# Moving a row norm with its read-back, one output product and the last output tile in a two-layer attention and gMLP kernel

## The chip, the cores and the metric

The kernel runs on one core of a Trainium2 chip. The metric is the device time of one execution in microseconds (us); less is better. Times are medians over several executions, and one execution is recorded by the hardware profiler.

In what follows PE is the matrix engine, DVE the vector engine, ACT the scalar engine, POOL the GpSimd engine and SP the engine whose queue issues most of the transfers. "L905" is line 905 of the kernel before the change.

## The reference

Two blocks are run twice over a sequence x of 2048 rows of 512 values, both as residuals. Block A is a recurrent attention with memory: 64 segments of 32 rows, each attending to itself and to 8 memory rows, which are the first 8 output rows of the segment before. Block B is a gated MLP with a spatial mixing over all 2048 rows.

```python
def A(x, mem, Wq, Wk, Wv, Wo):               # 32 heads of 128
    for s in range(64):
        h = concat([mem, x[32*s:32*s+32]])   # 40 rows
        q, k, v = h @ Wq, h @ Wk, h @ Wv
        o = softmax(mask(q @ k.T / sqrt(128))) @ v @ Wo
        mem = o[:8]; out.append(o[8:])
    return concat(out)

def B(x, w_in, w_sp, b_sp, w_out):
    z = gelu(x @ w_in)                       # 2048 x 1376
    g = w_sp @ layernorm(z[:, 688:]) + b_sp[:, None]
    return (z[:, :688] * g) @ w_out

x = x + A(layernorm(x));  x = x + B(layernorm(x))
x = x + A(layernorm(x));  x = x + B(layernorm(x))
```

## The kernel before

Four stages follow each other: `a_block` (first), `b_block`, `a_block`, `b_block` (last, which writes the output). Inside both, the order of the instructions on PE, DVE and ACT is the order of the code; in `b_block` SP's order is too, while in `a_block` SP's transfers are placed by a scheduler.

**Attention.** `segment(s, fill, spare1, spare2, tail)` issues one segment of 32 rows. Rows come in 16 blocks of 128 (`tb = s // 4`), so a block has four segments (`j4 = s % 4`). A segment projects its 40 rows (`hA`, transposed on DVE at L782) to q, k and v on PE, copies the results out of PSUM on ACT (L828, L844), transposes them on DVE (L832, L847), computes the scores, their exponentials (ACT, L872) and the masking (DVE, L875), the product with v (`psO`, L891) and the row sums (`psD`, L946). The memory rows are divided by their sums first (`uT<-psO,Rm`, L958) and multiplied with Wo (`pw`, L724), because the next segment needs them: `build_hA` puts them into the next segment's rows (L781) and transposes (L782). The other rows follow (`tok_out`, L905) once ACT has the reciprocal sums (`Rt`, L964). `fill()` puts matmuls of other work (the projections of each segment's last 8 rows, `b_units`, and earlier output products, `y_part`) into the places where PE would wait. The number of PE instructions of a segment is padded to a fixed multiple (`pads_of`).

Between these stand two places for work of other rows. `spare1` is called after the masking (L875) and ahead of L958, `spare2` after L958 and ahead of `tok_out`. In `spare1` stands the residual sum of an earlier row tile (`rows.y_add`), in `spare2` its statistics and the row norm of the tile two blocks ahead:

```python
                if j4 == 3 and tb + 2 < NB:
                    rows.apply(tb + 2, MV_in, RS_in, first=first)
```

`rows.apply` (L196) normalises 128 rows on DVE (L201) into `ln_xn`, stores them to `xn_d` in DRAM (L203), and reads them back in two layouts: four transfers into `preB` (L206) for `ahead.turn` and four tiles `pre` (L213), one for each segment of that block. It runs in 14 segments of each attention block. `rows.load` reads the rows for the next such call into the one buffer `ln_x`.

**gMLP.** `b_block` projects all 16 row tiles (`project`), normalises, and then mixes: `gate(t, sts)` multiplies the spatial weights of tile t (`wspT`, loaded transposed by `load_wsp` through SP) with all 16 row tiles, in two parts of 10 and 6 row tiles, 20 and 12 matmuls. `product(t)` multiplies the sum with the other half on DVE (L390), starts the load of the spatial weights of tile t + 3, transposes the product by a transfer (L394) to `uT[t]`, and loads the rows of tile t - 1 for the residual. `finish(t)` is the output product: six matmuls of 128x512 (L407), the residual sum on DVE (L412 in the last block, L415 in the first) and the store. PSUM tiles: `gate` uses `pg0` and the two slots of `two`, `finish` and `turn_u` the two slots of `one`. The sums `xo` have two buffers. `turn_u` transposes the last product on PE and copies it on ACT (L402), instead of by a transfer. The loop is

```python
        for t in range(3, NT):
            gate(t, range(0, 10))
            finish(t - 3)
            gate(t, range(10, NT))
            product(t)
```

and after it `finish(13)`, `turn_u(15)`, `finish(14)`, `finish(15)`.

Of the kernel before, what the change touches and what calls it, by code (L numbers as in the profile page):

```python
# [8 lines left out]
F32 = mybir.dt.float32  # L9
ACT = mybir.ActivationFunctionType  # L10
ALU = mybir.AluOpType
# [3 lines left out]
P = 128  # L15
DM = 512
# [20 lines left out]
def _perm(ap):  # L37

    return ap.rearrange("p (cg kt el) -> p kt cg el", cg=4, kt=4, el=32)


def _nat(ap):
    return ap.rearrange("p (kt cg el) -> p kt cg el", kt=4, cg=4, el=32)
# [77 lines left out]
def _rstd_act(nc, out, var, c):  # L121
    nc.scalar.activation(out=out, in_=var, func=ACT.Ln, bias=c["eps_t"][:], scale=1.0)
    nc.scalar.activation(out=out, in_=out, func=ACT.Exp, scale=-0.5)
# [19 lines left out]
def _stats(nc, pool, x_tile, MV_out_slot):  # L143
    st = pool.tile([P, nc.vector.BN_STATS_DIM], F32, name="bnst")
    nc.vector.bn_stats(out=st[:], in_=x_tile)
    nc.vector.bn_aggr(out=MV_out_slot, in_=st[:])
# [94 lines left out]
def b_block(tc, c, rows, front, xd, MV_out, RS_out, w_sp, w_out, S, first, ahead, wo, out_final=None):  # L241

    nc = tc.nc
    NT = S // P
    ident_bf = c["ident_bf"]
    with ExitStack() as ctx:

        def sbuf(name, stack=ctx, bufs=1):
            return stack.enter_context(tc.tile_pool(name=name, bufs=bufs))

        w_in_sb = front.w_in_sb
        w_out_sb = sbuf("b_w_out").tile([P, 6, DM], BF16, name="w_out_sb")
# [9 lines left out]
        xt, wsp = {}, {}  # L262

        def z(tt, lo=0, hi=FF):
            return zs[tt >= 6][:, tt - 6 * (tt >= 6), lo:hi]
# [99 lines left out]
        two = _Tagged(ps_pool, "two", 2)  # L365
        one = _Tagged(ps_pool, "one", 2)
# [3 lines left out]
        pg, u, uT, rstds = {}, {}, {}, []  # L370
        n = 6 * P
        us = [front.take(n * i, n) for i in range(2)]
# [4 lines left out]
        def gate(t, sts):  # L377
            if sts[0] == 0:
                pg[t] = (two if t % 3 else pg0).tile([P, 2, 512], F32, name="pg")
            for st in sts:  # L380
                for k in range(2):
                    nc.tensor.matmul(pg[t][:, k, 0:344], lhsT=wsp[t][:, st, :], rhs=z(st, 344 * k, 344 * k + 344),  # L382
                                     start=(st == 0), stop=(st == NT - 1))

        def product(t):
            del wsp[t]
            if t + 3 < NT:
                load_wsp(t + 3)
            u[t], uT[t] = us[t % 2], uTs[t % 3]
            nc.vector.scalar_tensor_tensor(out=u[t][:, 0:FH].rearrange("p (k f) -> p k f", k=2), in0=pg.pop(t)[:, :, 0:344],  # L390
                                           scalar=c["bsp"][:, t:t + 1], in1=z(t, FH).rearrange("p (k f) -> p k f", k=2),
                                           op0=ALU.add, op1=ALU.mult)
            if t + 1 < NT:
                nc.sync.dma_start_transpose(out=uT[t], in_=u[t].rearrange("t (fc s) -> t fc s", s=P))  # L394
            if t > 0:
                load_x(t - 1)

        def turn_u(t):
# [2 lines left out]
                nc.tensor.transpose(pT[:, fc * P:(fc + 1) * P], u[t][:, fc * P:(fc + 1) * P], ident_bf[:])  # L401
            nc.scalar.copy(uT[t].rearrange("p fc r -> p (fc r)"), pT[:, 0:n])  # L402

        def finish(t):
            py = one.tile([P, DM], F32, name="py")
            for fc in range(6):
                nc.tensor.matmul(py[:], lhsT=uT[t][:, fc, :], rhs=w_out_sb[:, fc, :], start=(fc == 0), stop=(fc == 5))  # L407
            xs = xt.pop(t)
            xo = gp.tile([P, DM], F32, name="xo")
            if out_final is not None:  # L410
                xob = xo[:, 0:DM // 2].bitcast(BF16)
                nc.vector.tensor_tensor(out=_nat(xob), in0=_nat(py[:]), in1=_perm(xs[:]), op=ALU.add)  # L412
                nc.sync.dma_start(out_final[t * P:(t + 1) * P, :], xob)
                return
            nc.vector.tensor_tensor(out=_perm(xo[:]), in0=_nat(py[:]), in1=_perm(xs[:]), op=ALU.add)  # L415
            nc.sync.dma_start(xd[t * P:(t + 1) * P, :], xo[:])
            _stats(nc, gp, xo[:], MV_out[:, t, :])
            rstds.append(lambda: _rstd_act(nc, RS_out[:, t:t + 1], MV_out[:, t, 1:2], c))
            if t < 2:
                rstds.pop()()  # L420
                rows.apply(t, MV_out, RS_out, x=xo[:], eng=nc.gpsimd)
            elif len(rstds) > 1:
                rstds.pop(0)()

        for t, sts, done in ((0, range(0, 10), False), (1, range(0, 10), False), (0, range(10, NT), True), (2, range(0, 10), False),
                             (1, range(10, NT), True), (2, range(10, NT), True)):
            gate(t, sts)
            if done:
                product(t)
        for t in range(3, NT):  # L430
            gate(t, range(0, 10))
            finish(t - 3)
            gate(t, range(10, NT))
            product(t)
            if t == NT - 2 and out_final is None:
                ahead.begin()
# [174 lines left out]
def a_block(tc, c, rows, front, MV_in, RS_in, MV_out, RS_out, ahead, wo, S, first):  # L611
    nc = tc.nc
    NSEG = S // SEG
    NB = S // P
# [3 lines left out]
    with ExitStack() as ctx:  # L618
# [55 lines left out]
        uT = [pers.tile([P, H, 32], BF16, name=f"uT{i}") for i in range(2)]  # L674
# [5 lines left out]
        def ln_turn(tb):  # L680
            blk_state[tb] = dict(hB=ahead.turn(tb), KTB=KTBr[tb % 2], QTB=QTBr[tb % 2], VB=VBr[tb % 2])
# [79 lines left out]
        def y_stats(tb):  # L761
            rows.y_stats(tb, MV_out[:, tb, :])
            copies.append(lambda: _rstd_act(nc, RS_out[:, tb:tb + 1], MV_out[:, tb, 1:2], c))
# [234 lines left out]
        def values(units):  # L998
            for n in (3, 1):
                for _ in range(n):  # L1000
                    next(units)
                run(copies)
                yield

        for s in range(NSEG):
            tb, j4 = s // 4, s % 4
            if j4 == 0:
                q = tb % 4
                more = y_part(tb // 4 - 1, range(8 * q, 8 * q + 8), (1, 2, 4), 4, q == 0, q == 3) if tb > 3 else iter(())
            if first and s == 0:  # L1010
                more = values(units)
            if j4 > 0 and tb == NB - 1:
                n = [sum(k) for k in TAIL_HEADS]
                stops = [sum(TAIL_HEADS[j4 - 1][:k]) for k in (1, 2, 3)]
                more = y_part(tb // 4, range(sum(n[:j4 - 1]), sum(n[:j4])), stops, 3, j4 == 1, j4 == 3)
            elif j4 == 1:
                more = b_units(tb + 1)
            if j4 == 1 and tb + 2 < NB:
                rows.load(tb + 2, first, nc.sync)

            def spare1():
                if first and s == 1:
                    ln_turn(1)
                if ys:
                    rows.y_add(ys[0], first, nc.vector, nc.sync)
                if s == NSEG - 1:
                    rows.y_load(due[0], first, nc.sync, rows.pool.tile([P, DM], F32, name="y_x")[:],
                                rowsB[:].rearrange("p a n -> p (a n)").bitcast(F32))()

            def spare2():  # L1030
                if first and s == 0:
                    rows.apply(1, MV_in, RS_in, first=True)
                if first and s == 8:
                    c["cast_bsp"] = c["load_bsp"]()
                if first and s == 12:
                    c["cast_bsp"]()
                if ys:
                    y_stats(ys[0])
                if j4 == 2 and tb + 2 < NB and first:
                    _stats(nc, rows.pool, rows.xs[tb + 2], MV_in[:, tb + 2, :])  # L1040
                    copies.append(lambda: _rstd_act(nc, RS_in[:, tb + 2:tb + 3], MV_in[:, tb + 2, 1:2], c))
                if j4 == 3 and tb + 2 < NB:
                    rows.apply(tb + 2, MV_in, RS_in, first=first)

            def tail():
                if j4 == 0 and tb + 1 < NB and not (first and s == 0):
                    ln_turn(tb + 1)
                if tb == NB - 1:
                    front.load_w(j4)
                    if j4 > 0:  # L1050
                        front.load_rows(j4 - 1)
                if ys:
                    y_norm(ys.pop(0), nc.sync)
                if tb % 4 == 3 and j4 == 0 and tb > 4:
                    due.extend(range(tb - 7, tb - 3))

                if due and (j4 != 3 or tb + 2 >= NB) and s < NSEG - 1:
                    ys.append(due.pop(0))
                    rows.y_load(ys[0], first, nc.sync)()

            segment(s, lambda: next(more, None), spare1, spare2, tail)
# [7 lines left out]
        for h in range(H):  # L1069
            n = h // 8 * 8 + 2 * (h % 4) + h // 4 % 2  # L1070
            for k in range(4):
                nc.tensor.matmul(pw[32 * k:32 * k + 32, 0:256], lhsT=ends[k // 2][:, n, :],
                                 rhs=wo.head(h).rearrange("p (kt g el) -> p g kt el", kt=4, g=4)[:, k % 2 * 2:k % 2 * 2 + 2],
                                 start=(h == 0), stop=(h == H - 1), tile_position=(0, 32 * k))
# [46 lines left out]
```

## Time and profile before

| | |
|---|---|
| median of 4 runs | 1775.41 us (1767.29 to 1777.56) |
| the profiled execution's own time | 1775.67 us |
| its span, first to last instruction | 1772.8 us |
| mean granted TensorE clock | 0.998 |
| first gate to the moved product, first gMLP | 802.4 to 819.5 us |
| the same in the last gMLP | 1672.6 to 1689.7 us |
| start of the last output sum (DVE L412) | 1769.36 us |

A row of the timeline gives the start, the duration, the engine, the line, the operation, the tiles with their shapes, the number of instructions merged into the row, and in brackets how long the engine had been idle and what released it. A row of the waits gives the total, the number and the longest. A row of the windows gives a stretch, its length, the busy time of PE, PEld (the weight loads), DVE, ACT and POOL with their numbers of instructions, the granted clock, the busy share of the transfer engines and GB/s.

### The profile page before, as it was taken

Reading aid. Unit: us, or ns where it says so; the run is one execution under the profiler, and the core shown is the slowest. Engines: PE = TensorE matmul, PEld = TensorE weight load, DVE = VectorE, ACT = ScalarE, POOL = GpSimd, SP = SyncE. Lnnn points to the kernel's source line nnn. Section 1 sums busy time; section 2 is a strip of 40 time slices with the busy share of each in tenths; the row PEclk is TensorE's granted clock in tenths of the full one; section 3 lists DMA queues with packets and bytes.
Section 4 is the critical chain, followed back from the end, with each engine's and each line's share of the span. In section 5 each row is a group of like instructions: output and inputs, shape, how many; then the busy total and the mean of one; then the engine's idle time right before and its main releaser. Section 6 shows DMA issues by size and latency. Waiting matters only on the chain.

```text
span 1772.8 us, 109760 instructions
## 1 busy us (share of the span) xinstructions
PE 1704.3 (96%) x51164; PEld 1275.5 (72%) x51164; DVE 1159.2 (65%) x2861; ACT 1110.3 (63%) x2274; POOL 121.9 (7%) x274
## 2 busy tenths in 40 slices
PE   2999999999999999999999999999999999999999
PEld 1677777777777777756667777777777777777565
DVE  2666666687667766775366666666776677666723
ACT  1677777777777777661057777777777777766500
POOL 6000000000000000021100000000000000001100
PEclk9999999999999999999999999999999999999999
DMA  9200000021002102277940000001210131114697
GB/s 353 65 20 20 20 20 20 20 73 44 18 17 67 54 25 42 80 161 162 208 138 23 23 21 23 23 23 41 80 38 23 35 89 42 31 30 144 136 184 171
DMA packets 191818, 124.53 MB, mean 70 GB/s; under 512 B 135961, under 2 KB 168057, under 8 KB 191361
## 3 DMA queue, kind: packets, MB, share of 16 engines
q1 hardware_dynamic: 182656, 90.37, 21.5%
q0 software_dynamic: 8688, 27.14, 4.6%
q8 instruction: 399, 6.54, 1.6%
q14 instruction: 59, 0.48, 0.1%
q10 hardware_dynamic: 16, 0.01, 0.0%
HBM read 57.06 MB, written 33.53 MB: 51 GB/s over the span
## 4 chain that ended last, share of the span: by engine, by line
PE 92%; DMA 3%; DVE 2%; issue 1%; POOL 1%; ACT 0%; DVEq 0%; SPq 0%; POOLq 0%
PE psm L667 14%; PE psV L667 14%; PE pw L724 13%; PE psm L841 12%; PE psb L667 10%; PE pg L382 8%; PE psS L865 5%; PE psO L891 4%; PE pwB L737 3%; PE pz L283 3%; PE py L407 2%; PE psD L946 2%; PE psM L937 2%; DMA Wo_high<-in_A_Wo_dram 1%; DMA Wv_sb<-in_A_Wv_dram 1%
## 5 line engine op out<-in xcount | busy, mean ns | idle before, releaser
L667 PEld LDWEIGHTS <-hA 128*32 128x32 bf16 x10960 | 358.2, 96 | 161.4 <-DVE hA L782 52.3
L667 PE MATMUL psV<-Wv_sb,hA 128*32 128x256 bf16 (+1 forms) x5791 | 288.6, 318 | 3.4 <-issue 3.0
L724 PEld LDWEIGHTS <-uT 128*32 128x32 bf16 x16384 | 234.1, 97 | 51.8 <-DVE uT L958 39.5
L841 PEld LDWEIGHTS <-hA 128*32 128x32 bf16 x8192 | 237.2, 97 | 0.9
L828 ACT CAST rows<-psm 128x512 bf16<-128x512 f32 x256 | 149.8, 585 | 136.7 <-PE psm L667 136.7
L905 DVE TENSOR_TENSOR uT<-psO,Rt 128x384 bf16<-128x384 f32 x256 | 140.7, 549 | 100.2 <-ACT Rt L964 100.2
L844 ACT CAST rows<-psm 128x256 bf16<-128x256 f32 x512 | 191.0, 374 | 17.0
L872 ACT ACTIVATE E<-psS 128x448 bf16<-128x448 f32 x256 | 125.7, 541 | 120.5 <-PE psS L865 120.5
L958 DVE TENSOR_TENSOR uT<-psO,Rm 128x128 bf16<-128x128 f32 x256 | 62.5, 285 | 182.2 <-PE psO L891 182.2
L964 ACT ACTIVATE Rt<-Rt 128x512 f32<-128x512 f32 x256 | 157.4, 629 | 4.0
L382 PE MATMUL pg<-z,wspT 128*128 128x344 bf16 x1024 | 154.5, 309 | 0.7 <-DMA wspT<-in_B_w_sp_dram 0.7
L667 PE MATMUL psm<-Wk_sb,hA 128*32 128x256 bf16 (+1 forms) x3121 | 147.0, 307 | 7.9 <-issue 7.3
L724 PE MATMUL pw<-Wo_high,uT 128*32 128x128 bf16 x8704 | 147.2, 219 | 1.0 <-DMA Wo_high<-in_A_Wo_dram 1.0
L724 PE MATMUL pw<-Wo,uT 128*32 128x128 bf16 x7680 | 140.8, 219 | 6.5 <-DVE uT L958 3.0
L667 PE MATMUL psm<-Wq_sb,hA 128*32 128x512 bf16 x2048 | 134.6, 382 | 7.7 <-DVE hA L782 7.6
L382 PEld LDWEIGHTS <-wspT 128*128 128x128 bf16 x1024 | 100.1, 98 | 54.1 <-DMA wspT<-in_B_w_sp_dram 1.0
L841 PE MATMUL psm<-Wk_sb,hA 128*32 128x256 bf16 x4096 | 137.0, 273 | 0.0
L841 PE MATMUL psm<-Wq_sb,hA 128*32 128x256 bf16 x4096 | 136.9, 273 | 0.0
L875 DVE TENSOR_TENSOR E<-E,maskN 128x448 bf16<-128x448 bf16 x256 | 104.3, 409 | 41.4 <-ACT E L872 39.2
L956 ACT ACTIVATE Rt<-psD 128x1024 f32<-128x1024 f32 x128 | 128.9, 1007 | 0.0
L667 PEld LDWEIGHTS <-hB 128*32 128x32 bf16 x2976 | 87.6, 97 | 48.6 <-DVE hB L582 22.8
L832 DVE STREAM_TRANSPOSE QQ<-rows 128x512 bf16<-128x512 bf16 x128 | 88.9, 694 | 34.4 <-ACT rows L828 34.4
(167 smaller groups left out, 2751.8 us busy)
## 6 DMA issues: line engine op xcount, KB each, us to landing
o_d<-o_sb SPq DMA_DIRECT2D x126, 64.0 KB
ln_x<-xd SPq DMA_DIRECT2D x26, 256.0 KB
y_o<-o_d SPq DMA_DIRECT2D x22, 256.0 KB
xd<-y_o SPq DMA_DIRECT2D x22, 256.0 KB
y_x<-xd SPq DMA_DIRECT2D x22, 256.0 KB
Wq_sb<-in_A_Wq_dram POOLq DMA_DIRECT2D x8, 512.0 KB, 6.4
Wk_sb<-in_A_Wk_dram POOLq DMA_DIRECT2D x8, 512.0 KB, 10.1
Wv_sb<-in_A_Wv_dram POOLq DMA_DIRECT2D x8, 512.0 KB, 11.9
```

The lines of the kernel that those rows point to most:

```text
L382: nc.tensor.matmul(pg[t][:, k, 0:344], lhsT=wsp[t][:, st, :], rhs=z(st, 344 * k, 344 * k + 344), start=(st == 0), stop=(st == NT - 1))
L667: nc.tensor.matmul(o, lhsT=lhs(kt, cg), rhs=r, start=(kt == 0 and a == 0), stop=(kt == KT - 1 or halved > 0), tile_position=(0, 32 * cg), ...
L724: nc.tensor.matmul(po[32 * cg:32 * cg + 32, 0:128], lhsT=lhs[:, n, :], rhs=wo_rhs(h, cg), start=(h == 0), stop=(h == H - 1), tile_position ...
L828: nc.scalar.copy(r[:], ps[:])
L832: nc.vector.transpose(out=QQ[:, j % 2, :, 0:32] if j < 2 else KA[:, j % 2], in_=r[:])
L841: nc.tensor.matmul(ps[32 * cg:32 * cg + 32, 0:256].rearrange("p (i c) -> p i c", i=2), lhsT=hA_cur[:, kt, :], rhs=qk_rhs(w, j, kt, cg)[:, ...
L844: nc.scalar.copy(r[:, 256 * a:256 * a + 256], ps[:, 0:256])
L872: nc.scalar.activation(out=E[:, r], in_=pS, func=ACT.Exp, scale=scale)
L875: nc.vector.tensor_tensor(out=E[:, r], in0=E[:, r], in1=maskN[:, j4, :].unsqueeze(1).to_broadcast([P, 4, 112]), op=ALU.mult)
L905: nc.vector.tensor_tensor(out=hview(uT_nxt[:], r, 8, 32), in0=oview(r, 8, 32), in1=r_view(r)[:, :, :, 0:24], op=ALU.mult)
L956: nc.scalar.activation(out=Rt[:], in_=psD[:], func=ACT.Ln)
L964: nc.scalar.activation(out=rt, in_=rt, func=ACT.Exp, scale=-1.0)
```

## The change

Three things move.

1. In a fourth segment (`j4 == 3`), `rows.apply` is called in `spare1`, behind a residual sum if there is one, instead of at the end of `spare2`. On DVE the norm (L201) then stands ahead of `uT<-psO,Rm` (L958) in 28 places; in four of them the statistics of a residual sum no longer stand ahead of it. On SP the store to `xn_d` passes one load of `y_x` in four places.
2. `finish(0)` is issued ahead of `gate(3, range(0, 10))` instead of behind it, in both gMLP blocks. On PE its six matmuls pass 20 gate matmuls. The order on the other engines stays.
3. In the last gMLP, `finish(13)` takes its PSUM tile from `two`, and `finish(15)` is replaced by `finish_last`, which computes two halves of 256 columns, each in a PSUM tile of `two`, with its own residual sum and store; the sums go to the space of the product `us[0]` instead of an `xo` buffer.

Over the whole program PE gets 12 instructions more, DVE one and SP one, all at the end.

```diff
+        def finish_last(t):
+
+            xs, xob = xt.pop(t), us[0][:, 0:DM]
+            for k in range(2):
+                cols = slice(256 * k, 256 * k + 256)
+                py = two.tile([P, 2, 512], F32, name="py2")[:, 0, 0:256]
+                for fc in range(6):
+                    nc.tensor.matmul(py, lhsT=uT[t][:, fc, :], rhs=w_out_sb[:, fc, cols], start=(fc == 0), stop=(fc == 5))
+                nc.vector.tensor_tensor(out=_nat(xob)[:, 2 * k:2 * k + 2], in0=py.rearrange("p (kt cg el) -> p kt cg el", kt=2, cg=4),
+                                        in1=_perm(xs[:])[:, 2 * k:2 * k + 2], op=ALU.add)
+                nc.sync.dma_start(out_final[t * P:(t + 1) * P, cols], xob[:, cols])
+
         def finish(t):
-            py = one.tile([P, DM], F32, name="py")
+
+            if t == NT - 1 and out_final is not None:
+                return finish_last(t)
+            if t == NT - 3 and out_final is not None:
+                py = two.tile([P, 2, 512], F32, name="py2")[:, 0, :]
+            else:
+                py = one.tile([P, DM], F32, name="py")[:]
             for fc in range(6):
-                nc.tensor.matmul(py[:], lhsT=uT[t][:, fc, :], rhs=w_out_sb[:, fc, :], start=(fc == 0), stop=(fc == 5))
+                nc.tensor.matmul(py, lhsT=uT[t][:, fc, :], rhs=w_out_sb[:, fc, :], start=(fc == 0), stop=(fc == 5))
...
         for t in range(3, NT):
+            if t == 3:
+                finish(0)
             gate(t, range(0, 10))
-            finish(t - 3)
+            if t > 3:
+                finish(t - 3)
             gate(t, range(10, NT))
             product(t)
...
                 if ys:
                     rows.y_add(ys[0], first, nc.vector, nc.sync)
+                if j4 == 3 and tb + 2 < NB:
+                    rows.apply(tb + 2, MV_in, RS_in, first=first)
...
-                if j4 == 3 and tb + 2 < NB:
-                    rows.apply(tb + 2, MV_in, RS_in, first=first)
```

## The prediction

> **What bounds the kernel now.** I read the page first: which engine is full, and what the chain that ended last consists of. Then the waits of PE over the whole span, because only a wait of PE (or the tail behind its last matmul) can give time back.
>
> ```profile
> PE 1704.3 (96%) x51164; PEld 1275.5 (72%) x51164; DVE 1159.2 (65%) x2861; ACT 1110.3 (63%) x2274; POOL 121.9 (7%) x274
> q8 instruction: 399, 6.54, 1.6%
> PE 92%; DMA 3%; DVE 2%; issue 1%; POOL 1%; ACT 0%; DVEq 0%; SPq 0%; POOLq 0%
> ```
>
> PE is busy 96% of the span and 92% of the chain. So each part of the change has to be asked: which wait of PE does it shorten? The list of PE's waits (total, times, longest, in us):
>
> ```profile
> PE psm L667 <- DVE hA L782: 7.6, 9, 1.6
> PE psm L667 <- issue: 7.3, 25, 0.6
> PE pw L724 <- DVE uT L958: 3.0, 8, 0.4
> PE py L407 <- DVE xo L412: 0.4, 1, 0.4
> ```
>
> By the timeline, the nine hA waits and the eight uT waits lie in the start-up and in first and second segments of a 128-row block (s % 4 of 0 and 1), none in a fourth segment, where the moved row norm sits. What fourth segments do lose is "issue": PE stands still with nothing to wait for. The starts of the hA transposition (L782) in the timeline are at best 10.79 us apart. Fourth segments average 11.18 us in the first attention block and 11.29 in the second, first ones 11.25 and 11.42 (without segment 0), second ones 11.25 and 11.37, third ones 11.11 and 11.18. The excess of 0.3 to 0.6 us comes at the same three places of a segment (about 2.3, 6.4 and 10 us after its hA); 399 instruction packets carry 6.54 MB, 16.4 KB each, so these are most likely instruction fetches that came late.
>
> **Part A, the row norm.** `rows.apply` moves from `spare2` to `spare1` in 28 fourth segments (14 per attention block): one DVE tensor_scalar, and its SP DMAs (one store to xn_d, four preB loads, four pre loads). One such segment:
>
> ```profile
> 170.02 0.83 DVE L875 TENSOR_TENSOR E<-E,maskN 128x448 bf16<-128x448 bf16 x2 [0.25 <-ACT E L872]
> 172.45 0.49 DVE L958 TENSOR_TENSOR uT<-psO,Rm 128x128 bf16<-128x128 f32 x2 [1.61 <-PE psO L891]
> 172.86 0.40 DVE L201 TENSOR_SCALAR ln_xn<-ln_x,MV,RS 128x512 bf16<-128x512 bf16 x1
> 174.03 0.56 DVE L905 TENSOR_TENSOR uT<-psO,Rt 128x384 bf16<-128x384 f32 x1 [0.77 <-ACT Rt L964]
> ```
>
> The norm (0.38 to 0.54 us) leaves a gap in which DVE waits 0.77 us more for ACT, and enters one in which DVE waits 1.61 us for PE. Neither wait ends sooner: L905 is released by ACT, L958 by PE. So DVE gives 0. In the four segments where a residual sum (L227, 0.69 us) precedes it, the wait ahead of L958 is 0.61 to 0.90 us and the norm takes 0.38 (first block) or 0.52; it still fits, by 0.1 to 0.4 us. If the cover were gone (the sum's load late, up to 0.9 us by its waits), L958 and with it the pw matmuls would slip at most about 0.5 us four times, 2 us.
>
> On SP the nine DMAs go some 2 us earlier (the norm starts at about 170.9 instead of 172.86):
>
> ```profile
> 173.29 0.33 SPq L203 DMA_DIRECT2D xn_d<-ln_xn  x1
> 175.06 3.09 SPq L206 DMA_DIRECT2D preB<-xn_d  x4
> 178.20 2.19 SPq L213 DMA_DIRECT2D pre<-xn_d  x4
> ```
>
> The next load of ln_x follows the store as before. The first reader of preB is the transposition at the end of the following segment, some 8 us after; that of pre is four segments away. Nothing waits for them now, so nothing is gained. Queued behind them on SP is the o_d store, which has no reader near; in four places the store passes a y_x load, which then waits for the norm, not needed before the next segment's sum. What remains is the burst itself against the instruction fetch. Here the page "Runtime: NRT & Kernel Launch" of the Trainium skill, section "Instruction fetch mechanics", says that crossing a 16 KiB block of instructions costs one queue bump, mostly hidden. By that rule A is exactly 0. The rows disagree: the issue gaps above, 0.3 to 0.6 us of excess per segment. So I bound A from the segments. Above 10.79, fourth segments lose 0.45 (mean of both blocks), second and third ones, with no burst, 0.44; first ones, where preB and pre land, 0.55. That is 0.11 x 26 = 3 us, some of it the uT waits. Gain at most 3 us. Loss: the store and the load of ln_x now precede the fetch needed at 10 us; if each of 28 segments gained a stall of the visible size, 0.3 us, 8 us. Nearest row is "no difference with or without the burst": I take 0.
>
> **Part B, the first output product** ahead of the fourth gate, once in each gMLP. Same six matmuls, 20 gate matmuls earlier.
>
> ```profile
> 814.82 4.83 PE L382 MATMUL pg<-z,wspT 128*128 128x344 bf16 x32
> 819.48 1.46 PE L407 MATMUL py<-w_out_sb,front 128*128 128x512 bf16 x6
> ```
>
> PE goes from the third gate into the fourth without a gap, so there is no wait to fill: gain 0. Gate matmuls start 0.147 us apart (116 of them from 1672.64 to 1689.74), so py moves from 819.48 to 816.5, and in the second block from 1689.74 to 1686.8. It then needs uT of tile 0, a DMA transposition issued at 812.38 (1682.70) behind the 512 KB of the fourth wspT. When it landed is not shown, but the windows show when its bytes ended:
>
> ```profile
> 814.50:815.00 0.50, 0.50 (x6) 0.33 (x4) 0.00 (x0) 0.00 (x0) 0.00 (x0) 1.00 1.03 228
> 815.00:815.50 0.50, 0.50 (x5) 0.36 (x4) 0.48 (x1) 0.00 (x0) 0.00 (x0) 1.00 0.00 0
> 1685.00:1685.50 0.50, 0.50 (x5) 0.33 (x4) 0.22 (x1) 0.00 (x0) 0.00 (x0) 1.00 0.69 157
> ```
>
> (last column GB/s): at 814.9 and 1685.3. Where PE did wait for a DMA transposition (pz at 1663.18), bytes ended about 1661.7, 1.5 us before. So uT is ready at about 816.4 and 1686.8: just in time. Bounds 0 and 0.5 us each; I take +0.1 each, +0.2. The DVE add behind py is released by its load of x (DVE xo <- DMA ln_x, until 822.16), the SP order stays, so product 3 and its wspT load stay. What is behind on PE if uT is late: the fourth gate, by the same amount.
>
> **Part C, the tail.** Output 13 goes to the pool of the gates, 15 into two halves, each with own bank, add and store.
>
> ```profile
> 1765.83 0.69 DVE L412 TENSOR_TENSOR xo<-py,y_x 128x512 bf16<-128x512 f32 x1 [0.36 <-PE py L407]
> 1766.20 0.80 ACT L402 COPY front<-pT 128x768 bf16<-128x768 bf16 x1 [92.05 <-PE pT L401]
> 1766.57 2.75 PE L407 MATMUL py<-w_out_sb,front 128*128 128x512 bf16 x12 [0.45 <-DVE xo L412]
> 1768.06 0.69 DVE L412 TENSOR_TENSOR xo<-py,y_o 128x512 bf16<-128x512 f32 x1 [1.54 <-PE py L407]
> 1769.36 0.69 DVE L412 TENSOR_TENSOR xo<-py,ln_x 128x512 bf16<-128x512 f32 x1 [0.60 <-PE py L407]
> ```
>
> Output 14 waits until the add of 13 frees its bank. After: no wait, it follows the six transpositions (the first at 1765.62, 56 ns apart) at 1766.0. Matmuls of 512 columns are 0.216 apart, so 14 ends at 1767.5, and 15 starts at 1767.3; its uT copy is done at 1767.0. Halves of 256 columns at 0.11: first half done 1767.3 + 0.55 + 0.27 = 1768.1, second 0.66 later, 1768.8. The half add: 691 ns at 512 columns and 549 at 384 (L905) give 0.41 by the line through both. Adds: 14 at 1767.5 to 1768.2, halves to 1768.6 and 1769.2, against 1770.05 now. **0.8 us.** The store after the last add takes 2.7 us to the end (1772.8) and has half the bytes; I leave it. Where this shrinks: x of tile 15 is issued at 1764.40, bytes end about 1766.7, plus 1.5 is 1768.2, just when the first half wants it. If it came 0.8 late, gain 0.2.
>
> A rule speaks against the halves: the page "TensorE: Matmul & The Clock Gate", section "LDWEIGHTS (loading the stationary operand)", puts a weight load at columns/1.2, 107 ns for 128, and its section "The mechanism" lets a load overlap a matmul only in another row group. Then twelve pairs of 107 + 109 end at 1770.1 and the last add at 1770.5, 0.4 us slower than now. The row for the six transpositions (0.50 us for six of 0.219, each with a full load) shows 56 ns between starts: loads hide. I keep 0.8.
>
> **Sum.** A 0, B +0.2, C -0.8: -0.6 us on a span of 1772.8 (1775.67 with what lies around it), so 1775.1 for that execution and 1774.8 against the median of 1775.41.
>
> **Rivals.** (1) Slower: the earlier xn_d store and ln_x load delay the instruction fetch at 10 us of fourth segments. 28 x 0.15 gives +4, 1779; with 0.3, 1783. For it: gaps of that size exist. Against: second segments without a burst stall as much. It decides from 0.02 us per segment on, where it eats the 0.6. (2) Faster: the burst leaves the next segment's fetch alone, -3: 1772. Against it: pre then lands where preB did. (3) The change doesn't do what it says: uT late twice by 0.5 and x of tile 15 late: +1.0 - 0.2 = 0.8 slower, 1776.2.
>
> **Numbers.** Forecast 0.63, rival 1 0.17, rival 2 0.12, rival 3 0.08. The four runs span 1767.3 to 1777.6, so a median may move by some 4 us on its own; range 1769 to 1781, which leaves out the far end of rival 1. A change under 0.5% (8.9 us) can't be told from none: same 0.93; slower 0.05 (rival 1 with more than 0.3), faster 0.02.
>
> **What would show it.** Right: L201 between L875 and L958 with L958 still released by PE; L905 still by ACT; fourth and first segments within 0.1 us of now; no wait before the moved py; py of 14 and 15 without a gap, the last add ending about 1.0 us after the add of 14 ends (1.3 now). Wrong: an issue or DVE wait of PE in fourth segments that wasn't there, their mean moved by over 0.2 us, or PE waiting for front before L407.

## The result, and the profile after

The changed kernel takes 1775.3 us (median of 43 runs, 1768.33 to 1782.49); the kernel before, run beside it, takes 1777.88 (64 runs, 1767.29 to 1786.9). The ratio is 0.9982, 95% interval 0.9972 to 0.9991: a gain of 3.2 us, between 1.6 and 5.0 (the medians themselves differ by 2.6). It is clear of noise, and a third of the 8.9 us that were set as the bound of "no change". The profiled execution has a span of 1771.8 us and took 1773.46, 1.0 and 2.2 us less than the profiled one of before. Single executions of one kernel lie up to 20 us apart, so what a part is worth has to be read from its own stage and from the experiments.

The page of the changed kernel, its busy times, instruction queue and chain:

```profile
PE 1703.9 (96%) x51170; PEld 1276.0 (72%) x51170; DVE 1159.9 (65%) x2862; ACT 1110.3 (63%) x2274; POOL 121.9 (7%) x274
q8 instruction: 400, 6.55, 1.6%
PE 91%; DMA 4%; issue 3%; POOL 1%; DVE 1%; ACT 0%; POOLq 0%; DVEq 0%; SPq 0%
```

Six matmuls and one DVE add more (the halves), one instruction packet more, and the same 96%. The waits of PE (total, times, longest):

```profile
PE psm L688 <- DVE hA L803: 7.6, 9, 1.6
PE psm L688 <- issue: 7.5, 23, 1.1
PE pw L745 <- DVE uT L979: 3.0, 8, 0.4
```

Lines of the attention block now stand 21 further down (L667 is L688, L782 is L803, L958 is L979). These three waits are what they were, to 0.2 us, and "PE py <- DVE xo" is gone: the last outputs no longer share a bank.

**Part A.** The timeline of the fourth segment shown before (here DVE, then SP):

```profile
170.90 0.82 DVE L896 TENSOR_TENSOR E<-E,maskN 128x448 bf16<-128x448 bf16 x2 [0.25 <-ACT E L893]
171.64 0.41 DVE L201 TENSOR_SCALAR ln_xn<-ln_x,MV,RS 128x512 bf16<-128x512 bf16 x1
173.21 0.49 DVE L979 TENSOR_TENSOR uT<-psO,Rm 128x128 bf16<-128x128 f32 x2 [1.16 <-PE psO L912]
174.79 0.56 DVE L926 TENSOR_TENSOR uT<-psO,Rt 128x384 bf16<-128x384 f32 x1 [1.09 <-ACT Rt L985]
```

```profile
172.08 0.33 SPq L203 DMA_DIRECT2D xn_d<-ln_xn  x1
174.40 3.08 SPq L206 DMA_DIRECT2D preB<-xn_d  x4
```

The norm has moved ahead of the uT pair. The pair's wait for PE shrinks from 1.61 to 1.16 us and still ends with PE's psO; the wait for ACT ahead of L926 grows from 0.77 to 1.09. The norm was taken out of one idle time and put into another. Fourth segments now average 11.15 and 11.19 us (11.18 and 11.29 before), first ones 11.14 and 11.49 (11.25 and 11.42), third ones, which the change leaves alone, 11.23 and 11.27 (11.11 and 11.18): a difference of 0.1 either way is what the trace scatters.

**Part B.** The moved output product of the first gMLP, and of the second:

```profile
818.10 1.46 PE L425 MATMUL py<-w_out_sb,front 128*128 128x512 bf16 x6
819.40 6.87 PE L382 MATMUL pg<-z,wspT 128*128 128x344 bf16 x46
1686.91 1.46 PE L425 MATMUL py<-w_out_sb,front 128*128 128x512 bf16 x6
```

Gate matmuls run up to it and on after it, and no wait stands at its row: uT of tile 0 was there.

**Part C.** The tail in the timeline:

```profile
1765.70 0.50 PE L401 MATMUL pT<-ident_bf,front 128*128 128x128 bf16 x6
1766.04 1.46 PE L425 MATMUL py<-w_out_sb,front 128*128 128x512 bf16 x6
1767.33 1.47 PE L411 MATMUL py<-w_out_sb,front 128*128 128x256 bf16 x12
1767.54 0.69 DVE L430 TENSOR_TENSOR xo<-py,y_o 128x512 bf16<-128x512 f32 x1 [0.94 <-PE py L425]
1768.19 0.42 DVE L412 TENSOR_TENSOR front<-py,ln_x 128x256 bf16<-128x256 f32 x1
1768.84 0.42 DVE L412 TENSOR_TENSOR front<-py,ln_x 128x256 bf16<-128x256 f32 x1 [0.23 <-PE py L411]
```

Output 14 (L425) follows the transpositions without a wait. From the first transposition of tile 15 to the end of the last add it is 3.56 us (1765.70 to 1769.26), before 4.43; from there to the end of the span 2.54 us, before 2.75. Together 6.10 in place of 7.18: 1.08 us. That the spans differ by as much is chance: ahead of the tail, stages differ by up to 1.4 us both ways (from the start of the last attention segment to the first gate it is 55.7 us in the first block and 53.9 in the second, before 54.3 and 55.3) and cancel to 0.1.

### The profile page after: what moved, and what is told of

It is laid out like the page before. It is cut to its first block, busy times and chain, and to the rows that moved or that the text cites. A ratio compares the mean times of both kernels' runs of the same rounds, so it can differ in the third digit from the quotient of the medians.

```text
span 1771.8 us, 109775 instructions
## 1 busy us (share of the span) xinstructions
PE 1703.9 (96%) x51170; PEld 1276.0 (72%) x51170; DVE 1159.9 (65%) x2862; ACT 1110.3 (63%) x2274; POOL 121.9 (7%) x274
## 4 chain that ended last, share of the span: by engine, by line
PE 91%; DMA 4%; issue 3%; POOL 1%; DVE 1%; ACT 0%; POOLq 0%; DVEq 0%; SPq 0%
PE psm L688 14%; PE psV L688 13%; PE pw L745 13%; PE psm L862 12%; PE psb L688 10%; PE pg L382 8%; PE psS L886 5%; PE psO L912 4%; PE pwB L758 3%; PE pz L283 2%; PE py L425 2%; PE psD L967 2%; PE psM L958 1%; DMA Wo_high<-in_A_Wo_dram 1%; DMA Wv_sb<-in_A_Wv_dram 1%
## 5 line engine op out<-in xcount | busy, mean ns | idle before, releaser
L688 PEld LDWEIGHTS <-hA 128*32 128x32 bf16 x10960 | 358.7, 96 | 160.4 <-DVE hA L803 52.1
L688 PE MATMUL psV<-Wv_sb,hA 128*32 128x256 bf16 (+1 forms) x5791 | 287.4, 318 | 2.2 <-issue 1.8
L926 DVE TENSOR_TENSOR uT<-psO,Rt 128x384 bf16<-128x384 f32 x256 | 140.7, 550 | 110.5 <-ACT Rt L985 110.5
L979 DVE TENSOR_TENSOR uT<-psO,Rm 128x128 bf16<-128x128 f32 x256 | 62.4, 285 | 167.7 <-PE psO L912 167.5
L688 PE MATMUL psm<-Wk_sb,hA 128*32 128x256 bf16 (+1 forms) x3121 | 148.3, 307 | 8.6 <-issue 7.5
L688 PE MATMUL psm<-Wq_sb,hA 128*32 128x512 bf16 x2048 | 134.6, 382 | 7.6 <-DVE hA L803 7.6
L688 PEld LDWEIGHTS <-hB 128*32 128x32 bf16 x2976 | 87.1, 97 | 50.2 <-DVE hB L603 25.5
L853 DVE STREAM_TRANSPOSE KA<-rows 128x512 bf16<-128x512 bf16 x128 | 90.6, 708 | 33.6 <-ACT rows L849 33.2
```

Source lines behind the costliest of these rows:

```text
L688: nc.tensor.matmul(o, lhsT=lhs(kt, cg), rhs=r, start=(kt == 0 and a == 0), stop=(kt == KT - 1 or halved > 0), tile_position=(0, 32 * cg), ...
L853: nc.vector.transpose(out=QQ[:, j % 2, :, 0:32] if j < 2 else KA[:, j % 2], in_=r[:])
L926: nc.vector.tensor_tensor(out=hview(uT_nxt[:], r, 8, 32), in0=oview(r, 8, 32), in1=r_view(r)[:, :, :, 0:24], op=ALU.mult)
```

## The experiments

Each kernel is compared with the kernel before in the same session, by its ratio. The kernel before itself took 1779.3, 1779.7, 1761.6 and 1749.8 us in the four sessions (1 and 3 on one chip, 2 and 4 on two others), so absolute times of different sessions aren't compared. "Tail" is the time from the first transposition of tile 15 to the end of the last add, plus the time to the end of the span, in the profiled execution.

| kernel | session | ratio, 95% interval | tail, us |
|---|---|---|---|
| changed kernel | own | 0.9982, 0.9972 to 0.9991 | 3.56 + 2.54 |
| e1: A alone | 1 | 0.9993, 0.9979 to 1.0006 | 5.34 + 2.67 |
| e2: B alone | 1 | 1.0000, 0.9985 to 1.0015 | 4.42 + 2.70 |
| e3: C alone | 1 | 0.9986, 0.9976 to 0.9996 | 3.55 + 2.52 |
| e5: norm later in place of earlier | 1 | 0.9999, 0.9984 to 1.0014 | 4.43 + 2.74 |
| e4: loads twice, old place | 2 | 1.0063, 1.0039 to 1.0087 | 4.43 + 2.68 |
| e6: changed kernel, last output whole | 2 | 0.9980, 0.9966 to 0.9994 | 5.10 + 2.73 |
| e7: PE stream shifted | 2 | 1.0111, 1.0087 to 1.0135 | 4.42 + 2.74 |
| e8: A and C | 2 | 0.9979, 0.9963 to 0.9994 | 3.56 + 2.49 |
| e9: own buffer alone | 3 | one run | 4.42 + 2.74 |
| e10: loads twice, new place | 3 | 1.0022, 1.0002 to 1.0043 | 5.52 + 2.70 |
| e12: loads left out | 3 | 0.9990, 0.9971 to 1.0008 | 4.42 + 2.76 |
| e11: as e4 | 4 | 1.0077, 1.0050 to 1.0104 | 4.43 + 2.75 |

### The parts one by one

e1, part A alone:

```diff
                 if ys:
                     rows.y_add(ys[0], first, nc.vector, nc.sync)
+                if j4 == 3 and tb + 2 < NB:
+                    rows.apply(tb + 2, MV_in, RS_in, first=first)
...
-                if j4 == 3 and tb + 2 < NB:
-                    rows.apply(tb + 2, MV_in, RS_in, first=first)
```

> The kernel before with part A alone (row norm, store and read-back in spare1 of fourth segments). The whole change measured a ratio of 0.9982 (about -3.2 us), while its traced tail is only 1.1 us shorter, so about 2 us are unexplained. Theory 1 (the prediction's): neither DVE wait ends sooner and the burst of transfers costs the same wherever it lies, so the ratio is 1.000 within 0.0006. Theory 2: the earlier burst leaves the instruction fetches alone, 2 us, ratio 0.9988, and the fourth and first segments of a block get shorter by 0.04 us each in the trace. Theory 3: the norm delays L979 or the burst delays the fetch, ratio above 1.0006.

Measured: 1777.21 beside 1779.26. The interval runs from -3.7 to +1.1 us; it excludes rival 1 beyond 1 us and can't tell 0 from a gain of 2 or 3. But its tail shows what the prediction didn't have. The timeline of e1:

```profile
1768.23 2.75 PE L407 MATMUL py<-w_out_sb,front 128*128 128x512 bf16 x12 [0.45 <-DVE xo L412]
1769.73 0.69 DVE L412 TENSOR_TENSOR xo<-py,y_o 128x512 bf16<-128x512 f32 x1 [1.54 <-PE py L407]
1771.94 0.69 DVE L412 TENSOR_TENSOR xo<-py,ln_x 128x512 bf16<-128x512 f32 x1 [1.52 <-DMA out_dram<-xo]
```

The last add waits 1.52 us for the store of an earlier output to leave its xo buffer (before: 0.60 for PE). Without that wait it would start 0.9 us earlier.

e2, part B alone:

```diff
         for t in range(3, NT):
+            if t == 3:
+                finish(0)
             gate(t, range(0, 10))
-            finish(t - 3)
+            if t > 3:
+                finish(t - 3)
```

> The kernel before with part B alone (first output product ahead of the fourth gate). Theory 1: PE ran from gate to gate without a gap, so nothing is gained; uT of tile 0 is there just in time, so at most 0.5 us twice is lost: ratio 1.000 to 1.0006, no wait of PE ahead of the moved py or one under 0.5 us. Rival: the two unexplained us come from here (a later gate no longer waits for its weights, the 0.7 us wait of pg for wspT in the first gMLP is gone): ratio 0.9989.

Measured: 1778.66 beside 1779.26, ratio 1.0000: nothing, within 2.7 us. The rival's wait of pg for its weights isn't gone: 1.1 us in e2's trace, 0.7 before.

e3, part C alone: `finish_last` and the py2 bank for tile 13, as in the changed kernel.

> The kernel before with part C alone (output 13 in the gates' bank, last output in two halves with own buffer). Theory 1: 0.8 us from the earlier last sum and 0.2 to 0.3 from the smaller last store, 1.1 us in all, ratio 0.9994. Rival: the tail is worth the whole 3.2 us because the end of the program (after the span) shortens too: ratio 0.9982 and a smaller difference between the execution's time and its span.

Measured: 1777.74, ratio 0.9986 (-0.7 to -4.3 us). Its tail is 3.55 + 2.52, as in the changed kernel. So the traced 1.1 us are part C's, and C alone accounts for a gain that may be all of it.

e8, parts A and C, B left as before:

> The changed kernel without part B (the first output product stays behind the fourth gate's first part). By the runs of the parts alone (norm 0.9993, first output 1.0000, tail 0.9986) the ratio is 0.9979 to 0.9985, the same as the whole change. Rival: the parts' point values are noise beyond the traced 1.1 us of the tail, ratio 0.9990 to 0.9995.

Measured: 1776.63 beside 1779.69, ratio 0.9979, -3.7 us (-1.1 to -6.6). With A it is 0.0007 under C alone, as the sum of the parts has it, but the intervals overlap by most of their width.

### The tail: banks, halves and buffer

e6 is the changed kernel with the last output in one piece and in an xo buffer:

```diff
-            if t == NT - 1 and out_final is not None:
-                return finish_last(t)
```

> The changed kernel without the halves: output 13 still goes to the gates' bank, but output 15 is one product of 512 columns with one sum in an xo buffer and one store. Theory 1: output 14 still starts right behind the transpositions (0.5 us earlier than in the kernel before), so from the first transposition to the end of the last sum 3.9 us instead of 4.43 (before) and 3.56 (changed), and 2.75 us from there to the end. Rival: the xo buffer of output 15 is that of output 13, and its store is the last wait; in the run of the row norm alone the last sum was released by that store 0.9 us after its product. Then the sum starts no earlier than before, 4.4 us or more.

Measured: ratio 0.9980, but the rival held, with 5.10 us to the end of the last add. The timeline shows the same wait as in e1, and longer, since tile 14 is done earlier:

```profile
1769.30 0.69 DVE L428 TENSOR_TENSOR xo<-py,y_o 128x512 bf16<-128x512 f32 x1 [0.94 <-PE py L423]
1771.88 0.69 DVE L428 TENSOR_TENSOR xo<-py,ln_x 128x512 bf16<-128x512 f32 x1 [1.89 <-DMA out_dram<-xo]
```

The freed bank alone gives the tail nothing: what PE saves, the last add spends waiting for the buffer. The tail is 1.7 us longer than the changed kernel's, and the ratio shows none of it: its interval is 5 us wide.

e9 takes the own buffer alone, without bank or halves:

```diff
-                xob = xo[:, 0:DM // 2].bitcast(BF16)
+                xob = us[0][:, 0:DM] if t == NT - 1 else xo[:, 0:DM // 2].bitcast(BF16)
```

> The kernel before, with one line of part C only: the last output's sum goes to a buffer of its own (us[0]) in place of an xo tile. No second bank, no halves. Theory: in a profile in which the sum of tile 15 isn't held up by the store of tile 13, this line gives nothing: first transposition of tile 15 to end of the last sum 4.43 us, as before, the sum released by PE (py) with about 0.6 us of wait, and 2.7 us from there to the end. So the 0.9 us of part C come from banks and halves, and the own buffer only takes away a wait that is there in some executions (1.5 us of idle time ahead of the last sum in the kernel with part A alone). Rival: the own buffer gives a part of the 0.9 us in every execution: 3.6 to 4.0 us in place of 4.43.

Measured: one run, 1764.27, and a tail of 4.42 us, with the last add released by PE:

```profile
1759.17 0.69 DVE L412 TENSOR_TENSOR front<-py,ln_x 128x512 bf16<-128x512 f32 x1 [0.60 <-PE py L407]
```

So the buffer alone gives nothing here; the 0.87 us (4.43 to 3.56) need bank and halves, which no run takes apart. The buffer gives something only where the store is late. When is it? Of the ten traces whose last add writes an xo tile, the three with the norm in the middle of the fourth segment (e1, e6, e10) have the wait, and the seven others (before, e2, e4, e5, e7, e11, e12) don't. The pages of the three have one instruction packet more; that of e1:

```profile
q8 instruction: 400, 6.55, 1.6%
```

(399 in each of the seven). The windows of the tail: two of e1, and the one of before that lies as far behind the first transposition (3.2 us) as e1's second (the last two columns are the share of the DMA engines and GB/s):

```profile
1770.00:1770.50 0.50, 0.50 (x4) 0.25 (x3) 0.42 (x1) 0.00 (x0) 0.00 (x0) 1.00 0.00 0
1770.50:1771.00 0.50, 0.48 (x3) 0.00 (x0) 0.00 (x0) 0.00 (x0) 0.00 (x0) 1.00 0.06 8
```

```profile
1768.80:1769.30 0.50, 0.50 (x3) 0.02 (x1) 0.00 (x0) 0.00 (x0) 0.00 (x0) 1.00 0.00 0
```

A share of 0.06 is one DMA engine of 16. In e1 it still moves some kilobytes when the rest of the store is done; before, nothing moves. The packets recorded in the traces show what it was doing. In e1 a 16 KB instruction packet lasts from 1769.22 to 1770.66 us. Of the 128 packets of tile 13's store (1 KB each) 120 have ended by 1769.57; the first of the other eight, a sixteenth of the store, starts at 1770.64. In e6 and e10 the instruction packet ends at 1770.59 and 1759.29, and the next store packet starts at 1770.58 and 1759.28. In all three the last add starts 1.28 to 1.32 us after the end of the instruction packet. So a sixteenth of the store stood behind an instruction packet, and the last add behind the store.

The changed kernel, e3 and e8 have the packet in the tail too, 1.3 to 1.4 us after the first transposition, and eight store packets behind it; with a buffer of its own no add waits for them. Since e3 has no part A, the buffer counts for C alone as well: with an xo buffer its first half would have started at about 1777.0 instead of 1776.01, an estimate from the 1.3 us above and the packet's end at 1775.73. In the other eight traces the packet comes over 7 us after the first transposition (in before at 1774.58, behind the span, so that the page counts one less), or there is none in the tail. Why it comes early in some kernels was not tried.

### The read-back: its place and its size

e5 moves the norm and its DMAs later than before, to the start of the segment's tail:

```diff
+
+            def tail():
                 if j4 == 3 and tb + 2 < NB:
                     rows.apply(tb + 2, MV_in, RS_in, first=first)
-
-            def tail():
```

> The kernel before with the row norm of fourth segments moved the other way, to the very end of the segment (tail), so that store and read-back come about 3.5 us later than before instead of 2 us earlier. Theory 1 (the place of the burst does not matter): ratio 1.000 within 0.0006. Theory 2 (the burst disturbs the instruction fetch by its place): a difference of 2 us or more, of the sign opposite to part A alone if the effect is monotonic; the norm then also stands ahead of the QQ and KA transpositions of the next segment, which would show as a PE wait ahead of psS.

Measured: 1779.59 beside 1779.26, 0.9999 (-2.8 to +2.5 us). In its timeline the norm starts 6.2 us after the mask product of the same segment (before 2.8): at its own size the burst can be 3.3 us later and cost no more than 2.5 us.

e4 leaves the place and doubles the eight loads:

```diff
-        for cg in range(4):
+        for cg in range(4 * times):
+            cg %= 4
...
+            for _ in range(times):
+                eng.dma_start(t[:], self.xn_d[t0:t0 + 32, :].rearrange("r (cg c) -> cg r c", cg=4))
```

> The kernel before with every read-back transfer of the 28 fourth segments' row norm issued twice (four preB and four pre loads more each, same data). It measures what such a burst costs by itself. Theory 1: next to nothing, PE's stalls come at every block of 256 instructions whether a burst is near or not; 224 more transfers cost under 1 us, ratio 1.000 within 0.0006. Theory 2 (the burst delays the instruction fetch): first segments of a block, into which the read-back falls, get longer by 0.1 to 0.3 us each, 3 to 8 us in all, ratio 1.002 to 1.0045.

Measured: 1.0063, 11 us (7 to 15.5) slower, more than either theory had. Part of it is a chain that the profile names. PE's waits of e4, and the place of the longest, SP first:

```profile
PE pw L726 <- DVE uT L960: 7.5, 10, 2.7
```

```profile
1235.90 2.20 SPq L215 DMA_DIRECT2D pre<-xn_d  x4
1238.20 0.54 SPq L790 DMA_DIRECT2D o_d<-o_sb  x1
1238.85 1.75 SPq L215 DMA_DIRECT2D pre<-xn_d  x3
1240.69 0.54 SPq L790 DMA_DIRECT2D o_d<-o_sb  x1
1241.29 0.60 SPq L732 DMA_DIRECT2D o_d<-yB  x1
1245.47 0.33 SPq L225 DMA_DIRECT2D y_o<-o_d  x1
```

```profile
1250.38 0.69 DVE L229 TENSOR_TENSOR y_o<-y_o,y_x 128x512 f32<-128x512 f32 x1 [4.08 <-DMA y_o<-o_d]
1251.33 1.79 PE L726 MATMUL pw<-Wo,uT 128*32 128x128 bf16 x60 [2.72 <-DVE uT L960]
```

Read down: the stores of o_sb and yB stand behind the loads on SP; y_o, the operand of the residual sum, is loaded after yB is stored; the sum sits ahead of uT on DVE, and waits 4.08 us; PE's pw matmuls wait 2.72 for uT. In the kernel before, the sum at this place waits 0.50 us and PE not at all. Two such places make 4.5 us of the 11 (7.5 against 3.0); of the rest the waits name some 3 us as issue gaps ("psm <- issue" is 10.5 us, before 7.3), and the remainder lies in first and second segments, where they name nothing.

e10 is part A and the doubled loads, at the new place:

```diff
-                    rows.apply(tb + 2, MV_in, RS_in, first=first)
+                    rows.apply(tb + 2, MV_in, RS_in, first=first, times=2)
```

> The kernel before with part A (the row norm in the middle of the fourth segment), and with the preB and pre loads of those 28 places issued twice. To be read against the doubled loads at the old place (1.0063 of before, +11 us, of which some 4 or 5 us were o_d and y stores held up behind the burst on SP). Theory 'the place is worth nothing': the same ratio, 1.0055 to 1.0065. Rival 'the early place keeps the burst clear of the stores at the segment's end': the store of o_d and the residual sum's store still come behind it on SP, but 2 us of the burst are over by then: 1.002 to 1.004, and the uT waits of PE (20 us in the doubled kernel, 3.0 before) fall under 8 us. If the rival holds, part A's own gain is real and about a quarter to a half of that difference, 1 to 3 us.

Measured: 1.0022, +3.9 us (0.4 to 7.6), and among PE's waits

```profile
PE pw L726 <- DVE uT L960: 3.0, 8, 0.4
```

as in the kernel before: the chain of e4 is gone. (The 20 us that the expectation gives for the doubled kernel are wrong; e4's trace has 7.5.) As the session ran faster, e4 was run again as e11:

> The same kernel as the one with the loads of preB and pre issued twice at the old place. It is run again because the kernel before itself took 1761.6 us beside the early doubled loads (1.0022) and 1779.7 beside the late ones (1.0063), so the two ratios were taken at different losses to instruction fetch. Theory 'the place of the burst matters': 1.0045 to 1.0075 again, above the early place's interval (1.0002 to 1.0043), whatever the kernel before takes beside it. Rival 'the doubled burst cost 11 us only because fetches were slow beside it': 1.001 to 1.0035 if the kernel before takes about 1762 us beside it; then the early place is worth nothing, and part A with it. If the kernel before takes about 1779 us, a ratio near 1.006 only repeats the first run and leaves this open.

Measured: 1763.93 beside 1749.82, 1.0077 (1.0050 to 1.0104), though the kernel before was the fastest of all sessions. Two ratios at the old place, 1.0063 and 1.0077, against 1.0022 at the new one: the place is worth 7 to 10 us when the burst is doubled. The intervals of e4 and e10 just touch, those of e11 and e10 don't. The chain of e4 is there again, at the same two segments: the sum waits 3.71 and 2.32 us, PE 2.35 and 1.37. It makes about 4 us of the difference; for the rest no trace names a cause ("psm <- issue" is 3.5 us here, 10.5 in e4).

e12 leaves the eight loads out: from the third block of rows on, segments use the tiles of the first two blocks.

> The kernel before without the read-back: from the third block of 128 rows on, segments use the preB and pre tiles of the first two blocks, so the eight loads of xn_d in those 28 places are left out (the norm and its store stay; rows 256 and on are computed from the first blocks' rows). It bounds what any place of the burst could be worth. Theory 'the burst costs PE only where it is doubled': 0 to -2 us, ratio 0.999 to 1.0, excess of segments over 10.79 us still 60 to 63 us. Rival 'each load costs PE, by delayed instruction fetches': as the doubling added some 6 us outside the waits for stores, leaving it out takes 5 to 8 us away, ratio 0.9955 to 0.997, and the excess falls to 54 to 57 us. Then moving the burst could be worth up to that, and the 2 us seen for part A are within it.

Measured: 1759.08 beside 1761.59, 0.9990 (-5.1 to +1.4 us). That bounds what any place can be worth at the burst's own size: 5 us, with 1.8 as the value measured. The theory's ratio held; its excess of 60 to 63 us can't be tested, as the session was faster (segments 1 to 62 of both blocks exceed 10.79 us by 42 us here and by 45 in e9, of the same session). The cost isn't linear: 1.8 us for the first burst, not told from 0, and 11 to 14 for the second.

### The gaps of PE that no semaphore explains

e7 leaves the row norm alone and moves PE's instruction stream:

```diff
-FILL_AHEAD = ((0, 0, 0, 106), (0, 0, 0, 42))
+FILL_AHEAD = ((0, 0, 0, 42), (0, 0, 0, 106))
```

That puts 60 PE instructions more into the zeroth segment of the first attention block and 60 fewer into that of the second.

> The kernel before with 60 PE instructions more in the first segment of the first attention block (30 products split in two) and 60 fewer in the first of the second, so that in the whole first attention block a boundary of 256 PE instructions falls 30 products earlier in a segment, and in the second where it was. If the 0.3 to 0.6 us that segments lose at three fixed places are instruction fetches, the three places move 30 products earlier in the first block only (the first from the second projection, 2.3 us after hA, to about 1.3 us), and the sum of the loss changes by up to 10 us either way. If they are something in the data path of those products, they stay.

Measured: 1799.96 beside 1779.69, 1.0111, 20 us slower. From the start of segment 1 to that of segment 63 the first block takes 718.4 us, before 694.2; the second, whose phase is as before, 702.0 and 701.4. PE's waits of e7:

```profile
PE psm L667 <- issue: 36.8, 71, 1.1
```

7.3 us before. A segment has 768 PE instructions, half of them weight loads, so it crosses three boundaries of 256. In the first block the gaps about 2.5 us after hA (9, together 2.4 us) are gone, and 56 of 30.5 us stand at 1.0 to 1.5 us, as forecast; in the second they stay at 2.5 (12 of 3.7 us, before 16 of 4.9). The size of the effect, 20 us, is twice the 10 that were expected at most.

The recorded packets tie these gaps to the fetches. The 14 traces have 651 gaps over 0.15 us that the profile puts down to issue; 648 of them end 1.2 to 1.65 us after the end of a 16 KB instruction packet, while such packets come at least 3 us apart. In before the end of a gap scatters less about the packet's end (0.10 us) than its beginning does (0.17 us). So in these traces PE goes on about 1.4 us after a block of instructions has come.

## Why the prediction was right, and where it wasn't

**The total.** Forecast 1774.8, measured 1775.3, and no difference by the bound of 0.5%. The size of the gain was too small: 0.6 against 3.2 (1.6 to 5.0). Since the kernel before measured 1777.88 beside it, and not 1775.41, part of the agreement in microseconds is luck; the ratio is the fairer test, and by it 1775.41 would have become 1772.2. That is the number of rival 2.

**Part C, -0.8, under-sized.** Its timing came out: the last add was forecast to end 3.58 us after the first transposition, it ended at 3.56, and 1.0 us after the add of 14, as forecast. What the prediction drew from the page "TensorE: Matmul & The Clock Gate" against the halves did not come: twelve half-width matmuls with full weight loads took 1.47 us, 0.12 apart, where it gave 0.22. "The store after the last add takes 2.7 us and has half the bytes; I leave it" was the first term too small: 0.2 us. The second was not seen at all: the last add's buffer can be held by an earlier store, by 0.9 us in a kernel with part A alone. x of tile 15 was in time.

**Part B, +0.2.** It is 0: no wait at either place, and 1.0000 alone. The estimate of 1.5 us from the end of the bytes to a usable transposition was near enough to say "just in time" and no nearer.

**Part A, 0, with the burst costing nothing.** On DVE every step held: the norm between the mask product and uT, both neighbours still released by PE and ACT. The step that failed is "queued behind them on SP is the o_d store, which has no reader near". It has one, over yB, the load of y_o, the sum and uT. At twice the size the chain held PE (4.08 us of wait on DVE, 2.72 on PE); at the burst's own size it had cover enough: before, PE's only waits for uT are eight in first segments, and the changed kernel has the same eight. So this chain gave part A nothing.

Whether part A is worth anything with one burst isn't settled. If the tails of the traces hold for all executions, what each kernel gains outside its tail is: 2.1 us for the changed kernel (0.5 to 3.9), 2.1 for A alone (-0.2 to 4.6), 2.6 for e8 (0 to 5.5), and 4.2 for e6 (1.7 to 6.7), whose tail is 0.65 us longer than before's. These point to some 2 us for part A rather than to 0. Against it, e3, which has no part A, leaves 1.4 us (-0.4 to 3.2), and no stage of the traces is shorter in all kernels with part A. The cause of this remainder stays open.

**The rivals.** Rival 1 (earlier loads delay the fetch, +4 or more) is excluded: A alone is +1.1 at most, fourth segments did not grow, and even doubled the early burst costs 3.9. Rival 2 (-3) has the right number by the ratio; its mechanism isn't seen, since first segments of the changed kernel lose 0.35 and 0.70 us over 10.79 in the two blocks, before 0.46 and 0.63. Rival 3 (late uT and x) didn't happen. The reading behind all of them, that PE's gaps in the segments are instruction fetches, was confirmed by e7 and the packets. By the page "Runtime: NRT & Kernel Launch", section "Instruction fetch mechanics", the crossing of a block of instructions is mostly hidden; here the gaps listed as issue sum to 14 us in before and to 41 in e7, which is 20 us slower. The whole excess of segments 1 to 62 of both blocks over 10.79 is 57.6 us in before: 8 of them are waits for hA and uT, 14 issue, and for over 30 the trace names nothing.

## What to carry to other kernels

When a burst of small transfers moves on a queue, follow the stores behind it to their last reader, over memory and back: "no reader near" is a claim about a chain and not about one tile. A freed bank at the end of a kernel is worth only as much as the next resource in the row leaves, here an output buffer; take both. Where a part is worth less than the runs can tell, double it: the difference between places, lost at one burst, stood out at two. But what stands out then holds for two: the chain that cost PE 4 us there cost it nothing at one.

## What the hardware showed unasked

- The position of PE's instructions counts: 60 more in one segment made the following 62 segments 24 us longer, with the work and the data the same.
- An instruction packet can hold up data: in six traces eight of the 128 packets of a store started only when a 16 KB instruction packet had ended, in e1 1.07 us after the other 120 were done, and where the store's buffer was needed the kernel's end waited.
- The same program lost different amounts in its segments in different sessions, on one chip too (sessions 1 and 3). The excess of segments over 10.79 us is 57.6 us in the trace of before (span 1772.8) and 45.5 in that of e9 (1762.6), which differs from it by one line at the very end; the granted clock was 0.998 and 0.997.
- Doubling 28 bursts of eight small loads cost 11 to 14 us at the old place and 4 us two microseconds earlier; leaving them out gave 1.8, not told from 0.
